# Routing digits and comparison results laid out token tile by token tile, with each digit written twice

## The chip, the core and the metric

The kernel runs on one core of a Trainium2 chip. The metric is the device time of one execution in microseconds (us); lower is better. TensorE (PE) multiplies matrices, VectorE (DVE) and ScalarE (ACT) work element by element, GpSimd (POOL) does some of that and the indirect DMAs, and SyncE's queue (SP) issues most other DMAs. Each engine takes its instructions in order from its own queue and waits on semaphores.

## The reference

Three stages follow one another. Attention: 4 batches, 8 heads, 576 positions, head dimension 64, half of the heads with a local window of 32, half with a strided mask. Its output is the x of 2304 tokens by 512. Then a layer with a cosine gate, and then a mixture of 8 experts whose tokens are assigned greedily under a capacity of 288:

```python
h = x @ w_in
x = (h * np.cos(h)) @ w_out
logits = x @ w_gate                          # 2304 x 8
order = np.argsort(-logits.flatten())
for idx in order:
    tok, e = idx // E, idx % E
    if assigned[tok] >= 0 or counts[e] >= cap:
        continue
    assigned[tok] = e
    counts[e] += 1
for e in range(E):
    mask = assigned == e
    out[mask] = np.maximum(x[mask] @ w1[e], 0.0) @ w2[e]
```

## The kernel before, in words

Tokens lie in 18 tiles of 128 (NC = 18): token 128 c + p is partition p, column c. Products of float32 accuracy are made of three float16 products (high and low parts). The instructions are first put into a plan (`Plan`, line 159) as groups with an engine, a nominal time, and the buffers that they read and write. `Plan.order` (line 192) simulates the engines on these nominal times and writes out one fixed list per engine; of the groups that could start, an engine takes the one with the longest way to the end. What the chip then does is wait, not choose. All matmuls go through `mm` (line 343, recorded as L358), all VectorE work through `Vec` (line 387, recorded as L392), activations through `act` (L382).

The stretch that matters here is the routing (`route`, line 1021), between the last logits and the first gather. The greedy assignment is done in 7 phases (loop over `ph`, line 1088), and each finds the logit at which one expert is full. In a phase:

- `best()` (line 1079) finds each token's best open expert; `oh` is its one-hot code (line 1090). It is copied 16 times side by side into `ohr` [128, NC, 16, NE], tiles 0 to 11 on VectorE (line 1091) and 12 to 17 on ScalarE (line 1092), so that `ohr[:, c]` is a stationary operand of 128 columns.
- The threshold is found digit by digit, 5 times (NIT, loop over `it`, line 1097). `d` holds one float16 digit per token (lines 1096 and 1114), `io` the 34 digit values (NDIG) to compare with, built once (line 1087). The compare `gq` (line 1099) says for every token and digit value whether the token's digit reaches it: 34 x 18 = 612 elements per partition.
- The product (line 1106): 18 matmuls, one per token tile, each with `ohr[:, c]` as the stationary and `gq[:, :, c]` as the moving operand (34 columns), add up in PSUM how many tokens of each expert reach each digit value. In the old layout [NDIG, NC] the 34 elements of a tile lie 18 elements apart.
- VectorE compares the counts with the room left (line 1108; in the trace TENSOR_SCALAR_CACHE_REDUCE and DVE_READ_ACCUMULATOR), transposes and takes the maximum (lines 1110 and 1111), and computes the next digit (line 1114). Here the next step begins. The result of the compare goes from VectorE to TensorE, that of the product back to VectorE, and so on: a chain.
- After the fifth digit, lines 1120 to 1143 settle ties and mark the expert as full.

Between the routing's products TensorE's list holds the second layer of the cosine stage (`l2_tile`, line 986): per token tile 48 products of up to 128 rows with 512 columns, tiles 5 to 17, in groups of `L2_GROUP` = 2 matmuls. They fill the time in which the chain is on VectorE. Their results are scaled on ScalarE, split on VectorE or GpSimd, and stored as `y_dram`.

In the same stretch `expert_weights` (line 1190) brings weights through two staging buffers `wst`: a DMA of 512 KB on SP, then for each half a rounding to float16 on ScalarE (line 1205) and the rest by a subtraction on VectorE (line 1206, SCALAR_TENSOR_TENSOR 128x512). A buffer is loaded again when both halves are subtracted. Expert 0's weights come at the routing's beginning, expert 1's at its end, since they take the memory of a part of the hidden layer. Expert 0's tokens are gathered (line 1219) when the routing has written the indices `idx` (line 1184).

Of the kernel before, what the change touches and what calls it, by code (L numbers as in the profile page):

```python
# [11 lines left out]
F16 = mybir.dt.float16  # L12
# [5 lines left out]
ALU = mybir.AluOpType  # L18
# [4 lines left out]
B, H, S, D = 4, 8, 576, 64  # L23
# [28 lines left out]
# changes of priority, by label  # L52
# [43 lines left out]
# engines that differ from the first one offered at a place  # L96
# [62 lines left out]
class Plan:  # L159
    """Instructions in groups, each on one engine, with the buffers that they read and write.  # L160
    order() lists them by a simulated schedule: of the groups that could start, an engine takes
    the one with the longest way to the end."""

    # from the end of a group to the start of one that needs it
# [42 lines left out]
    def reuse(self, old, new):  # L207
        """Buffers whose names start with one of `new` take the memory of those of `old`."""
        keys = [k for k in self.writer if k[0] in old]
        i = self.add(None, 0.0, None, w=keys)  # L210
        for k in keys:
            del self.writer[k], self.readers[k]
        for n in new:
            self.base[n] = i
        return i

    def order(self):
# [41 lines left out]
        def pe_end(i, at):  # L259
            """TensorE's clock is halved after a window with little activity, until one with much"""  # L260
            warm_ns = t[i][1]
            cold_ns, a = self.busy[i]
            left = 1.0
            while left > 1e-9:
                win = int(at / self.WINDOW + 1e-9)
                look(win)
                ns = warm_ns if warm[win] else cold_ns
                dt = min(left * ns, (win + 1) * self.WINDOW - at)
                active[win] += (a if warm[win] else 2.0 * a) * dt / ns
                left -= dt / ns  # L270
                at += dt
            return at
# [62 lines left out]
def kernel(ctx: ExitStack, tc: tile.TileContext, a: dict, out: bass.AP):  # L335
# [4 lines left out]
    # ------------------------------------------------------------ instructions  # L340
    def mm(group, r, w):
        """group: (out, lhsT, rhs, start, stop) each"""
        ns = cold = act_ns = 0.0
        for o, l, x, _, _ in group:
            k, m, n = l.shape[0], l.shape[1], size(x)
            if x.dtype == F32:
                one = 0.88 * n + 19.5 if k == 64 else max(n, m) / 0.6 * (1.0 if m > 64 else 0.76)
                cold += 2.0 * one
                act_ns += n / 0.6 * (1.0 if m > 64 else 0.5) * k / 128.0
            else:  # L350
                one = n / 9.6 + 15.0 if m <= 32 < n else n / 4.8 + 12.5 if m <= 64 < n else max(n / 2.4 + 3.0, 25.0)
                cold += max(2.0 * one - 6.0, 27.0)
                act_ns += n / 2.4 * k / 128.0
            ns += one

        def emit():
            for o, l, x, start, stop in group:
                nc.tensor.matmul(o, l, x, start=start, stop=stop)  # L358

        p.add("pe", ns, emit, r, w, busy=(cold, act_ns))  # L360
# [26 lines left out]
    class Vec:  # L387
        """Calls on the vector engine: dve.op(n, keys read, keys written, *args)"""
# [9 lines left out]
    def choose(site, *engines):  # L398
        """the engine of a place in the program: the first one named if CHOICE has no other"""
        return CHOICE.get(site, engines[0])  # L400

    def vtt(site, o, x, y, op, r, w, first="pool"):
        """a tensor_tensor on Pool or DVE"""
        if choose(site, *(("pool", "dve") if first == "pool" else ("dve", "pool"))) == "pool":
            ptt(o, x, y, op, r, w)
        else:
            dve.tensor_tensor(size(o), r, w, o, x, y, op=op)

    def low(site, o, x, scale, hi, xk, r, w, first="pool"):
        """o = scale * x - hi; on Pool it leaves scale * x in x"""  # L410
        if choose(site, *(("pool", "dve") if first == "pool" else ("dve", "pool"))) == "pool":
            pscale(x, x, scale, r, xk)
            ptt(o, x, hi, ALU.subtract, r, w)
        else:
            dve.scalar_tensor_tensor(size(o), r, w, o, x, scale, hi, op0=ALU.mult, op1=ALU.subtract)
# [7 lines left out]
    def ecopy(site, o, x, r, w, *engines):  # L423
        """a copy on the first of the engines if CHOICE has no other"""
        how = choose(site, *engines)
        if how == "pool":
            p.add("pool", 146.0 + 3.28 * size(o), lambda: nc.gpsimd.tensor_copy(o, x), r, w)
        elif how == "dve":
            dve.tensor_copy(size(o) // (2 if site[0] == "og" else 1), r, w, o, x)
        else:  # L430
            acopy(o, x, r, w)
# [10 lines left out]
    def dma_t(o, x, r, w):  # L442
        """16-bit transpose of blocks of 128 columns"""
        p.add("sp", 112.0 * x.shape[1] / 128, lambda: nc.sync.dma_start(o, x, transpose=True), r, w)

    # ------------------------------------------------------------------ memory
# [58 lines left out]
    # the clock of TensorE rises before the first products  # L505
# [3 lines left out]
    # --------------------------------------------------------------- attention  # L509
# [59 lines left out]
    def masks(pv, i0, i1, np_, local, o=2 * LK):  # L569
        """the start of a bank of scores: 8 times the mask"""  # L570
# [10 lines left out]
    def softmax(b, pr, scores, pv, sbk, halves, sv, sk, scale, norm):  # L581
        """sv = norm * softmax(scale * scores), keys sk + (0 or 1,)"""
# [106 lines left out]
    def att_half_load(b, pr):  # L689
        """as att_load, and the operands in float16 parts"""  # L690
# [18 lines left out]
    def att_half(b, pr):  # L709
        """att_pair with products of float16 parts"""  # L710
# [84 lines left out]
    # ----------------------------------------------------------------- weights  # L795
    def to_f32(site, dst, words, sk, ck):
        """The float32 of float64 given as its two 32-bit words."""
# [72 lines left out]
    # --------------------------------------------------------------- layer one  # L870
# [54 lines left out]
    def g_segments(t0, n):  # L925
        """tokens t0 .. t0+n-1 as (tile, offset, length, keys of a layer unit)"""
# [10 lines left out]
    # ------------------------------------------------------------------ logits  # L937
    def logits(c0, take, after=()):
        """gate logits of tokens 128 c0 .. 128 c0 + 383, straight from the hidden layer"""
# [22 lines left out]
    def early_logits(c, ys, yi, take):  # L962
        """gate logits of tokens 128 c .. 128 c + 127 from their rows of y; the rows are transposed into a free part of x"""
# [19 lines left out]
    # --------------------------------------------------------------- layer two  # L983
    yss, yfs = [], []

    def l2_tile(c, take, nf=2):
        """y rows 128c .. 128c+127, in float16 parts"""
# [32 lines left out]
    # ----------------------------------------------------------------- routing  # L1020
    def route(take, take_t):
        """Greedy assignment under the capacity: in every phase the tokens left go, best logit
        first, to their best open expert until one expert is full; the phase finds the logit at
        which that happens.  Then the tokens of each expert get slots, and idx their inverse."""

        def t(name, shape, dt=F32):
            return take(shape, dt)
# [42 lines left out]
        ds = [t("d", [128, NC], F16) for _ in range(2)]  # L1070
        eq, oh = t("eq", full), t("oh", full, F16)
        nt, nm, ne = t("nt", [128, 32]), t("nm", [128, 1]), t("ne", [128, 1])
        reach, io = t("reach", [128, NDIG]), t("io", [128, NDIG, NC], F16)
        gqs = [t("gq", [128, NDIG, NC], F16) for _ in range(2)]
# [12 lines left out]
        D(TS, 612, ["cb"], ["io"], io, cb[:, RC_J:RC_J + NDIG, None].to_broadcast([128, NDIG, NC]), 1520.0, None, op0=ALU.add)  # L1087
        for ph in range(NE - 1):
# [4 lines left out]
            # the logit of the token that fills an expert, digit by digit: the float16 of 1536 + x  # L1093
            # has x rounded to a whole number, -16 .. 16 in the part of the range that is looked at
            di, d = rot("d", ds)
            D(TS, NC, ["m"], [("r", "d", di)], d, m, 32.0, 1536.0, op0=ALU.mult, op1=ALU.add)
            for it in range(NIT):
                gi, gq = rot("gq", gqs)
                D(TT, 306, [("r", "d", di), "io"], [("gq", gi)], gq, d[:, None, :].to_broadcast([128, NDIG, NC]), io, op=ALU.is_ge)
# [6 lines left out]
                mm([(pc[:, :NDIG], ohr[:, c].rearrange("p a b -> p (a b)"), gq[:, :, c], c == 0, c == NC - 1) for c in range(NC)],  # L1106
# [5 lines left out]
                if it + 1 < NIT:  # L1112
                    di, d = rot("d", ds)
                    D(TS, 66, ["u", "nm"], [("r", "d", di)], d, u, nm, -32.0, op0=ALU.add, op1=ALU.mult)
# [8 lines left out]
            D(TS, 66, [("r", "d", di), "nm"], ["tie"], tie, d, nm, 1519.0, op0=ALU.subtract, op1=ALU.is_equal)  # L1123
            D(RED, NE, ["ce"], ["e8"], e8, ce, axis=AX.X, op=ALU.max)
            D(TT, 1, ["rem", "cv"], ["rem"], rem, rem, cv, op=ALU.subtract)
            D(TS, 66, [("r", "d", di), "nm"], ["sure"], sure, d, nm, 1520.0, op0=ALU.subtract, op1=ALU.is_ge)
# [62 lines left out]
    # ----------------------------------------------------------------- experts  # L1189
# [123 lines left out]
    # ---------------------------------------------------------------- the plan  # L1313
# [198 lines left out]
```

## Time and profile before

| | us |
|---|---|
| three runs | 814.16 (median), 814.12, 816.64 |
| span of the profiled execution | 813.8 |
| its routing, from the first digit product to the index product | 399.35 to 575.82 |

The profile's page gives no time of the profiled execution beside its span, which goes from its first to its last instruction; the median of the runs is 0.36 us above it. Stages are read best from a table of busy time per stretch. A row of a timeline gives the start, the length, the engine, the line, the operation, what it writes and reads, and how many consecutive instructions are merged into it. A matmul's recorded duration contains its way through the array, so consecutive ones overlap: the time from start to start is the merged length less the last one's duration, divided by the count less one.

### The profile page before, as it was taken

How to read it: one execution, taken by the hardware profiler on the slowest of the kernel's cores; microseconds unless marked ns; L12 is line 12 of the kernel's file. 1: busy time of each engine (PE TensorE's matmuls, PEld its weight loads, DVE VectorE, ACT ScalarE, POOL GpSimd, SP SyncE). 2: the span in 40 equal slices, each digit the busy share in tenths (PEclk: the TensorE clock that was granted, in tenths of full speed). 3: DMA queues.
4: the chain of work that ended last, by engine and by line, in shares of the span. 5: the costliest groups of instructions: out<-in, count | busy, mean ns of one | idle time of the engine just before them, and what ended most of it. 6: DMA issues, size and time to landing. Idle time of an engine off the chain costs nothing.

```text
span 813.8 us, 18700 instructions
## 1 busy us (share of the span) xinstructions
PE 739.8 (91%) x7520; PEld 519.7 (64%) x7520; DVE 527.3 (65%) x1356; ACT 410.9 (50%) x907; POOL 277.2 (34%) x292
## 2 busy tenths in 40 slices
PE   7878888989889989999999999999899989888896
PEld 5666666755444767877555565445787767666685
DVE  5899999984856788555685655458435556544620
ACT  3557778865734889788220000023135554554632
POOL 2766466856520364344010000000531343231231
PEclk9999999999999999999999999999999999999998
DMA  9954155654766722002330000006498999978731
GB/s 262 271 163 145 53 134 128 155 130 122 156 159 166 169 48 62 2 1 64 105 130 14 28 14 14 14 14 183 128 186 213 241 257 218 224 234 227 177 70 40
DMA packets 114262, 104.14 MB, mean 128 GB/s; under 512 B 79872, under 2 KB 89856, under 8 KB 114176
## 3 DMA queue, kind: packets, MB, share of 16 engines
q1 hardware_dynamic: 111104, 93.52, 45.0%
q0 software_dynamic: 3072, 9.44, 3.9%
q8 instruction: 59, 0.97, 0.5%
q14 instruction: 27, 0.22, 0.1%
HBM read 74.36 MB, written 9.70 MB: 103 GB/s over the span
## 4 chain that ended last, share of the span: by engine, by line
PE 40%; DMA 21%; DVE 20%; ACT 11%; issue 4%; POOL 3%; SPq 0%; POOLq 0%; DVEq 0%; ACTq 0%
PE psum L358 38%; DMA ar_l<-w 14%; DVE ar_t L392 7%; DVE ar_l L392 7%; ACT ar_l L382 5%; DVE ar_a L392 2%; ACT ar_t L382 2%; DVE ar_w L392 2%; ACT ar_a L382 2%; DMA ar_l<-ar_t 1%; DMA ar_a<-q 1%; DVE mxs L392 1%; DMA ar_w<-ar_w 1%; DMA ar_t<-w_out 1%; ACT L382 1%
## 5 line engine op out<-in xcount | busy, mean ns | idle before, releaser
L358 PEld LDWEIGHTS <-ar_l 128*128 128x128 f16 x2576 | 234.9, 100 | 102.4 <-issue 35.4
L358 PE MATMUL psum<-ar_l 128*128 128x288 f16 (+2 forms) x1578 | 206.9, 287 | 20.0 <-DVE ar_l L392 19.5
L358 PEld LDWEIGHTS <-ar_a 128*128 128x128 f16 (+1 forms) x1600 | 128.4, 99 | 90.4 <-issue 36.5
L358 PE MATMUL psum<-ar_w,ar_a 128*128 128x512 f16 (+3 forms) x1056 | 173.9, 308 | 6.3 <-DVE ar_w L392 2.8
L382 ACT ACTIVATE ar_l<-psum 128x288 int32<-128x288 f32 (+5 forms) x201 | 78.5, 413 | 111.7 <-PE psum L358 97.9
L358 PEld LDWEIGHTS <-ar_t 128*128 128x128 f16 (+2 forms) x1980 | 97.0, 107 | 43.5 <-issue 18.5
L392 DVE SCALAR_TENSOR_TENSOR ar_l<-ar_l,psum 128x288 f32<-128x288 int32 (+2 forms) x236 | 98.0, 440 | 34.4 <-ACT ar_l L382 33.1
L382 ACT ACTIVATE ar_a<-ar_l 128x512 f16<-128x512 f32 (+2 forms) x125 | 63.6, 537 | 55.6 <-DMA ar_l<-w 50.5
L392 DVE SCALAR_TENSOR_TENSOR ar_l<-ar_l 128x512 f16<-128x512 f32 (+3 forms) x94 | 52.3, 576 | 33.4 <-ACT ar_l L382 32.6
L382 ACT ACTIVATE ar_l<-ar_l,quarter 128x288 f32<-128x288 f32 x128 | 66.2, 531 | 13.0 <-DVE ar_l L392 12.2
L392 DVE SCALAR_TENSOR_TENSOR ar_t<-ar_t 128x512 uint32<-128x512 uint32 (+6 forms) x60 | 61.9, 1034 | 14.1 <-ACT ar_t L382 14.1
L437 POOL TENSOR_TENSOR ar_l<-ar_l 128x288 f32<-128x288 f32 (+1 forms) x41 | 27.8, 680 | 119.2 <-DVE ar_l L392 89.0
L392 DVE SCALAR_TENSOR_TENSOR ar_a<-ar_l,ar_a 128x512 f16<-128x512 f32 x64 | 43.5, 710 | 36.1 <-ACT ar_a L382 36.1
L358 PE MATMUL psum<-ar_w,ar_t 128*128 128x512 f16 (+2 forms) x288 | 65.4, 357 | 0.0
L382 ACT ACTIVATE ar_l<-ar_l 128x512 f16<-128x512 f32 x64 | 37.0, 622 | 53.3 <-DMA ar_l<-w 53.2
L382 ACT ACTIVATE ar_t<-ar_t 128x512 uint32<-128x512 uint32 (+12 forms) x63 | 46.4, 755 | 34.4 <-DVE ar_t L392 10.0
L358 PE MATMUL psum<-ar_b,ar_l 128*128 128x96 f16 (+1 forms) x576 | 54.4, 259 | 8.7 <-ACT ar_b L382 4.9
L358 PE MATMUL psum<-ar_w,ar_b 128*128 128x512 f16 (+1 forms) x240 | 61.5, 388 | 0.0
L358 PE MATMUL psum<-ar_b,ar_a 128*128 128x288 f16 (+3 forms) x504 | 53.4, 272 | 4.9 <-DVE ar_w L392 3.8
L358 PE MATMUL psum<-ar_w,ar_l 128*128 128x288 f16 x384 | 49.6, 292 | 3.8 <-DVE ar_w L392 3.8
L1296 POOL DMA_INDIRECT out<-ar_b,idx x24 | 23.5, 979 | 85.0 <-DMA out<-ar_b,idx 19.1
L392 DVE SCALAR_TENSOR_TENSOR ar_w<-psum,ar_w 128x288 f16<-128x288 f32 x64 | 28.0, 451 | 32.0 <-ACT ar_w L382 31.7
(142 smaller groups left out, 915.6 us busy)
## 6 DMA issues: line engine op xcount, KB each, us to landing
ar_l<-w SPq DMA_DIRECT2D x64, 512.0 KB
ar_t<-w_out SPq DMA_DIRECT2D x16, 512.0 KB
ar_t<-w_in SPq DMA_DIRECT2D x12, 512.0 KB
y_dram<-ar_l SPq DMA_DIRECT2D x13, 256.0 KB
ar_t<-vl SPq DMA_DIRECT2D x6, 432.0 KB
ar_t<-qs SPq DMA_DIRECT2D x4, 648.0 KB
ar_t<-vs SPq DMA_DIRECT2D x6, 384.0 KB
ar_t<-ql SPq DMA_DIRECT2D x4, 576.0 KB
```

What stands on the lines that cost most here:

```text
L358: nc.tensor.matmul(o, l, x, start=start, stop=stop)
L382: p.add("act", ns, lambda: nc.scalar.activation(o, x, func, **kw), r, w, tab=tab)
L392: p.add("dve", 69.0 + 1.042 * n, lambda: getattr(nc.vector, name)(*args, **kw), r, w)
L437: p.add("pool", 145.0 + (rate or (1.667 if y.dtype == F32 else 1.885)) * size(o), lambda: nc.gpsimd.tensor_tensor(o, x, y, op=op), r, w)
L1296: p.add("pool", 546.0, lambda og=og, T=T: nc.gpsimd.indirect_dma_start(out[:, :], bass.IndirectOffsetOnAxis(ap=idx[:, T:T + 1], axis=0), o ...
```

## The change

The layout of the table `io` and of the compare results `gq` becomes [NC, NDIG], token tile by token tile, so that the moving operand `gq[:, c, :]` is 34 elements in one piece. The digits `d` become [NC, 2]: each is written twice side by side, from an operand that is read with each element repeated (`twice`). The compare reads `d` as [NC, 17, 2], with the pair of equal digits repeated 17 times, and `gq` and `io` as 17 pairs per tile (`pairs`). The two later uses of the digits read every other element. The nominal times of the two digit instructions grow by 18 and by 18 elements. Blank lines also take the place of comments, which is left out here.

```diff
@@ route @@
-        ds = [t("d", [128, NC], F16) for _ in range(2)]
+        ds = [t("d", [128, NC, 2], F16) for _ in range(2)]
...
-        reach, io = t("reach", [128, NDIG]), t("io", [128, NDIG, NC], F16)
-        gqs = [t("gq", [128, NDIG, NC], F16) for _ in range(2)]
+        reach, io = t("reach", [128, NDIG]), t("io", [128, NC, NDIG], F16)
+        gqs = [t("gq", [128, NC, NDIG], F16) for _ in range(2)]
...
-        D(TS, 612, ["cb"], ["io"], io, cb[:, RC_J:RC_J + NDIG, None].to_broadcast([128, NDIG, NC]), 1520.0, None, op0=ALU.add)
+        D(TS, 612, ["cb"], ["io"], io, cb[:, None, RC_J:RC_J + NDIG].to_broadcast([128, NC, NDIG]), 1520.0, None, op0=ALU.add)
+        pairs = lambda x: x.rearrange("p c (j h) -> p c j h", h=2)
+        twice = lambda x: x[:, :, None].to_broadcast([128, NC, 2])
         for ph in range(NE - 1):
...
-            D(TS, NC, ["m"], [("r", "d", di)], d, m, 32.0, 1536.0, op0=ALU.mult, op1=ALU.add)
+            D(TS, 2 * NC, ["m"], [("r", "d", di)], d, twice(m), 32.0, 1536.0, op0=ALU.mult, op1=ALU.add)
             for it in range(NIT):
                 gi, gq = rot("gq", gqs)
-                D(TT, 306, [("r", "d", di), "io"], [("gq", gi)], gq, d[:, None, :].to_broadcast([128, NDIG, NC]), io, op=ALU.is_ge)
+                D(TT, 306, [("r", "d", di), "io"], [("gq", gi)], pairs(gq),
+                  d[:, :, None, :].to_broadcast([128, NC, NDIG // 2, 2]), pairs(io), op=ALU.is_ge)
...
-                mm([(pc[:, :NDIG], ohr[:, c].rearrange("p a b -> p (a b)"), gq[:, :, c], c == 0, c == NC - 1) for c in range(NC)],
+                mm([(pc[:, :NDIG], ohr[:, c].rearrange("p a b -> p (a b)"), gq[:, c, :], c == 0, c == NC - 1) for c in range(NC)],
                    [("gq", gi), ("fit", 0), ("fit", 1)], kc)
...
-                    D(TS, 66, ["u", "nm"], [("r", "d", di)], d, u, nm, -32.0, op0=ALU.add, op1=ALU.mult)
+                    D(TS, 2 * NC + 48, ["u", "nm"], [("r", "d", di)], d, twice(u), nm, -32.0, op0=ALU.add, op1=ALU.mult)
...
-            D(TS, 66, [("r", "d", di), "nm"], ["tie"], tie, d, nm, 1519.0, op0=ALU.subtract, op1=ALU.is_equal)
+            D(TS, 66, [("r", "d", di), "nm"], ["tie"], tie, d[:, :, 0], nm, 1519.0, op0=ALU.subtract, op1=ALU.is_equal)
...
-            D(TS, 66, [("r", "d", di), "nm"], ["sure"], sure, d, nm, 1520.0, op0=ALU.subtract, op1=ALU.is_ge)
+            D(TS, 66, [("r", "d", di), "nm"], ["sure"], sure, d[:, :, 0], nm, 1520.0, op0=ALU.subtract, op1=ALU.is_ge)
```

## Rows read from the trace of the kernel before

**Rows 1.** The page's busy time per engine: us, share of the span, instructions.

```profile
PE 739.8 (91%) x7520; PEld 519.7 (64%) x7520; DVE 527.3 (65%) x1356; ACT 410.9 (50%) x907; POOL 277.2 (34%) x292
```

**Rows 2.** Busy time by stretch, of the routing; columns as in the first row.

```profile
core 0: us, PE busy (x) PEld busy (x) DVE busy (x) ACT busy (x) POOL busy (x), PEclk, DMA share, GB/s
395.00:575.80 180.80, 178.16 (x1313) 98.45 (x1313) 119.25 (x535) 31.47 (x53) 12.49 (x21) 1.00 0.20 65
```

**Rows 3.** The chain of waits in order of time: start, us, what; its longest pieces.

```profile
393.06 45.59 PE psum L358 x340
...
442.12 114.28 PE psum L358 x850
```

**Rows 4.** Matmuls by shape, 385 to 600 us: busy us, mean ns, idle before.

```profile
L358 PE MATMUL psum<-ar_l,ar_t 128*128 128x34 f16 x630 | 45.6, 242 | 0.0
...
L358 PE MATMUL psum<-wp,ar_t 128*128 128x16 f16 x52 | 3.3, 172 | 0.0
L358 PE MATMUL psum<-wp,ar_t 128*128 128x8 f16 x52 | 3.2, 166 | 0.0
```

**Rows 5.** Timeline of one search step, 449.5 to 453.1 us.

```profile
449.75 1.31 PE L358 MATMUL psum<-ar_l,ar_t 128*128 128x34 f16 x18
...
450.88 2.34 PE L358 MATMUL psum<-ar_w,ar_a 128*128 128x512 f16 x10
451.10 0.25 DVE L392 TENSOR_SCALAR_CACHE_REDUCE ar_l<-psum,ar_l 128x33 f32<-128x33 f32 x1 [0.97 <-PE psum L358]
...
451.87 0.35 DVE L392 TENSOR_SCALAR ar_l<-ar_l 128x18 f16<-128x18 f32 x2
452.14 0.48 DVE L392 TENSOR_TENSOR ar_l<-ar_l 128x612 f16<-128x612 f16 x1
...
453.06 0.22 PE L358 MATMUL psum<-ar_l,ar_t 128*128 128x34 f16 x1
```

**Rows 6.** Timeline of TensorE: logits (16 and 8 columns in turn) and expert 0 (96 columns).

```profile
267.40 0.34 PE L358 MATMUL psum<-wp,ar_b 128*128 128x16 f16 x8
...
584.06 2.04 PE L358 MATMUL psum<-ar_b,ar_l 128*128 128x96 f16 x44
```

**Rows 7.** The chain of waits, 540 to 600 us.

```profile
558.24 3.99 DMA ar_l<-w
...
562.91 0.69 DVE ar_a L392
...
564.45 4.67 DMA ar_l<-w
...
569.81 0.69 DVE ar_a L392
...
575.16 0.62 DVE ar_l L392
575.78 0.04 issue
575.82 5.69 PE psum L358 x46
```

**Rows 8.** VectorE by shape, 395 to 578 us: busy us, mean ns, idle before.

```profile
L392 DVE TENSOR_TENSOR ar_l<-ar_l 128x612 f16<-128x612 f16 x35 | 16.7, 477 | 0.3
...
L392 DVE TENSOR_TENSOR ar_l<-ar_l 128x144 f32<-128x144 f32 x16 | 4.9, 303 | 0.2
...
L392 DVE TENSOR_TENSOR ar_t<-ar_t 128x1728 f16<-128x1728 f16 x1 | 1.9, 1944 | 0.0
```

**Rows 9.** Timeline of a phase's beginning, 425 to 455 us.

```profile
445.34 0.83 ACT L385 COPY ar_t<-ar_l 128x768 f16<-128x768 f16 x1 [5.15 <-DVE ar_l L392]
...
446.45 1.30 PE L358 MATMUL psum<-ar_l,ar_t 128*128 128x34 f16 x18
```

**Rows 10.** Timelines of VectorE, ScalarE and TensorE in the last phase.

```profile
550.36 0.68 DVE L392 SCALAR_TENSOR_TENSOR ar_a<-ar_l,ar_a 128x512 f16<-128x512 f32 x1
...
556.82 0.69 DVE L392 SCALAR_TENSOR_TENSOR ar_a<-ar_l,ar_a 128x512 f16<-128x512 f32 x1
...
556.16 1.15 ACT L382 ACTIVATE ar_a<-ar_l 128x512 f16<-128x512 f32 x2 [1.81 <-DMA ar_l<-w]
...
551.97 1.31 PE L358 MATMUL psum<-ar_l,ar_t 128*128 128x34 f16 x18
```

## The prediction, made before the change was timed

> **What bounds the kernel now.** I read the page's busy shares first, then the busy time of stages, the chain of waits, and last the timeline of one search step. The page says that TensorE is busy for 91% of an 813.8 us span [rows 1]. That is an average; the change touches only the routing, so the stage is what counts. [...] The chain of waits runs through TensorE alone for 45.59 us and then for 114.28 us in this stretch [rows 3]. So while the routing searches for its thresholds, TensorE's queue ends last: it holds the layer-two products of the cosine layer and, slipped in between them in a fixed order, the routing's own products. What shortens TensorE's list in this stretch shortens the kernel, as long as the routing's chain on VectorE stays within what TensorE has to do anyway.
>
> **What the routing costs TensorE.** There are 7 phases of 5 digit searches, so 35 products of 18 matmuls with 34 columns: the 630 rows of the group [rows 4]. One product begins at 449.75 and the layer-two matmul behind it at 450.88 [rows 5]: 1.13 us for 18 matmuls, 0.063 each. Its moving operand is read with a step of 18 elements (36 bytes), since a column of one token tile is strided in the old layout. The 35 products take 39.6 us of TensorE.
>
> How fast could such a matmul be? In the kernel's logits, matmuls of 16 and 8 columns, read without a gap and each with a fresh 128x128 stationary operand, run as a group of eight in 0.34 us, of which the last one's duration is 0.17: 0.17 / 7 = 0.024 us from start to start [rows 4, 6]. Matmuls of 96 columns without a gap, also with a fresh 128x128 operand, run 44 in 2.04 us with some 0.21 for the last one: 0.043 each [rows 6]. Thirty-four columns lie near 16 and far from 96, and the time of neither is proportional to its columns. I take 0.025. A product is then 18 x 0.025 = 0.45, and 0.04 for the change to the next 512-column matmul: 0.49 us in place of 1.13, a saving of 0.64. With 0.043 each it would be 0.81 and the saving 0.32. The bounds are thus nothing and 0.64 us a product; the least is what remains if the stride is not the cause.
>
> [...] The rows show 0.063 us a matmul for 34 strided columns and 0.024 for 16 in one piece. [...]
>
> **What the change costs VectorE.** One search step, followed through [rows 5]: the last matmul of the product starts at 450.82 (449.75 + 1.31 less its own 0.24), VectorE's comparison with the room left starts at 451.10, and after the transpose, the maximum and the new digit (451.87) the 612-element compare ends at 452.62. The next product starts at 453.06. TensorE needs 0.05 us from the end of a VectorE result to its start (575.78 to 575.82, where it stood idle) [rows 7]. So the step's chain has 453.06 - 452.62 - 0.05 = 0.39 us to spare under ten layer-two matmuls (2.34 us in the timeline, the last one overlapping). Of the 28 steps inside phases 19 have this pattern, the others have 12 to 16 matmuls there.
> - Digits written twice: 18 to 36 elements, between nothing and 18 x 1.1 ns, the dearest rate below: 0.02 us at most. It is in the chain, so in the slack. I take 0.02.
> - The compare: the number of elements is the same. Now it takes 0.477 us [rows 8], with the digit row of 18 read again and again. A compare whose one operand repeats each single element takes 1.944 us for 1728 elements, 1.125 ns each [rows 8], so 0.69 for 612. The paired digits keep an innermost run of two elements; I take 0.48, with 0.69 as the upper bound: 0.21 more, still inside the 0.39. A gain is excluded as far as the time goes: the chain is covered.
> - The product's last matmul also ends sooner: 34 columns in one piece should last about as long as the logits' 16 (0.17) rather than 0.242 [rows 4], so the chain begins some 0.06 earlier. Slack and gain grow together.
> - The table of comparison digits is built once, before the routing, and the two reads of every other digit at a phase's end are 18 elements as before: nothing, under layer-two work.
> - The first product of a phase waits for the repeated one-hot copies; ScalarE's ends at 446.17 and the product starts at 446.45 [rows 9]. The compare ended long before. Nothing changes there.
> No DMA, no wait and no queue position is added. The list order is computed from nominal costs, which grow by 19 ns per digit; a pair of layer-two matmuls may move by one step, which leaves TensorE's sum as it is.
>
> **What is late next.** Of the 35 products 33 lie before VectorE's subtraction at 550.36 us, and two behind it (551.97 is the first) [rows 10]: 33 x 0.64 = 21.1 us. Behind that, expert 1's weights get into the chain: two staging buffers, each loaded, rounded by ScalarE and subtracted by VectorE in VectorE's fixed order, with the routing's last steps queued behind the subtractions. Already now the subtraction at 556.82 begins the moment its ScalarE half is there (556.16 and 0.6), and the loads of 3.99 and 4.67 us follow in the chain with the subtractions at 562.91 and 569.81 [rows 7, 10]. The load that the subtraction at 556.82 waits for could be issued only once the one at 550.36 had emptied its buffer, so the saving of the two last products (1.3 us) finds the weights no earlier: I keep 0.06 of it, from the earlier start of the chain. In phase 0, where expert 0's weights share VectorE in the same way, I take off 0.3, a guess between nothing and one step's 0.64. Sum: 21.1 + 0.06 - 0.3 = 20.9 us. From 575.8 on nothing has a fixed start: gathers, expert weights and stores are released by what came before, so the rest moves as a block. Against the span that gives 813.8 - 20.9 = 792.9 us. The median of the runs is 814.16, 0.36 above the profiled span, so I predict 793.3 us.
>
> **Rivals.**
> - Partial: a matmul keeps 0.043 us, the figure of 96 columns [rows 6]. Then 35 x 0.32 = 11.2 us, less 0.6 at the weights: 814.16 - 10.6, about 803.5. Against it: 34 is far nearer to 16. Chance 0.06.
> - Nothing: 0.063 has another cause than the stride, a floor of issue for instance, and the change does not do what it says on TensorE. The compare stays in its slack, so 814.2. Against it: the 0.024 of the logits in the same queue [rows 6]. [...] Chance 0.06.
> - Slower, by one mechanism: the compare has to start anew at each of its 306 pairs. In a step the chain would then be product 0.45, about 1.73 from the last matmul's start to the compare's end, 0.05, and the excess x: 2.23 + x, against 3.31 us from start to start now (449.75 to 453.06). It decides from x = 1.08 us, so from 0.69 + 306 r - 0.48 = 1.08, r = 2.8 ns a pair. At 5 ns x is 1.74 and 28 steps lose 0.66 each: 814.2 + 18.5 = 832.7. Against it: a multiplication in rows of 8 takes 0.303 us for 144 elements [rows 8], with no visible charge per row; no row shows rows of two. Chance 0.03.
>
> **How the numbers follow.** My forecast has 0.85, the partial rival 0.06, no change 0.06, slower 0.03. Faster by over 0.3% (2.4 us, about what a measurement of this kernel can tell from no change) is 0.85 + 0.06 = 0.91; same 0.06; slower 0.03. The low end takes 35 full savings with nothing given back (22.4 us) and 0.06 in some twenty steps (1.2 us): 790.5. The high end takes the forecast with 0.030 us a matmul (35 x 18 x 0.005 = 3.2 us less), 1.5 us more lost at the weights of experts 0 and 1 (what I take off there, once more), and 2.0 us for a list whose pairs fall out worse (five pairs of 0.43 us: ten matmuls take 2.18 us from 450.88 to 453.06 [rows 5]): 800. The other three cases, 0.15 together, stay outside.
>
> **What would show it.** The 34-column group should fall from 0.242 to about 0.18 us a matmul, and a product from 1.13 to 0.5 us; the compare should stay at 0.48 us and the ten 512-column matmuls follow at once, with TensorE never idle inside a phase; the step should be some 2.67 us; the index product should come near 555 us. More waiting of VectorE for the weights of expert 1 should appear at the end of the routing. I am wrong on TensorE if the product keeps 1.1 us, and wrong on VectorE if the compare exceeds 0.87 us, for then gaps open before the products.

## The result, and the profile after

The changed kernel takes 795.37 us (median of four runs, 794.81 to 796.68), the kernel before in the same session 815.4: a ratio of 0.976 with a 95% interval of 0.9725 to 0.9796. Measured twice more beside the experiments it is 0.9736 [0.9685, 0.9788] and 0.973 [0.9686, 0.9774]. The forecast of 793.3 for 814.16 is a ratio of 0.974, so faster, and by about as much as forecast.

Read in the order of the prediction: first the page's busy shares of the kernel after, to be held against [rows 1].

```profile
PE 717.5 (90%) x7520; PEld 497.4 (63%) x7520; DVE 527.4 (66%) x1356; ACT 409.7 (52%) x907; POOL 275.7 (35%) x292
```

TensorE has lost 22.3 us of work (739.8 to 717.5) and VectorE none (527.3 to 527.4), with the same counts of instructions. The next view, matmuls by shape from 385 to 600 us, says where; it answers to [rows 4].

```profile
L358 PE MATMUL psum<-ar_l,ar_t 128*128 128x34 f16 x630 | 21.3, 178 | 0.6 <-DVE ar_l L392 0.6
...
L358 PE MATMUL psum<-wp,ar_t 128*128 128x16 f16 x52 | 3.4, 174 | 0.0
L358 PE MATMUL psum<-wp,ar_t 128*128 128x8 f16 x52 | 3.3, 167 | 0.0
```

The 630 digit matmuls fell from 242 to 178 ns each, and as a group from 45.6 to 21.3 us; the logits' 16 and 8 columns beside them did not move. The timeline of two search steps (start, length, engine) shows the rest; it answers to [rows 5].

```profile
449.70 0.61 PE L358 MATMUL psum<-ar_l,ar_t 128*128 128x34 f16 x18
...
450.16 2.32 PE L358 MATMUL psum<-ar_w,ar_a 128*128 128x512 f16 x10
450.35 0.25 DVE L392 TENSOR_SCALAR_CACHE_REDUCE ar_l<-psum,ar_l 128x33 f32<-128x33 f32 x1 [0.55 <-PE psum L358]
...
451.11 0.36 DVE L392 TENSOR_SCALAR ar_l<-ar_l 128x36 f16<-128x36 f32 x2
451.39 0.48 DVE L392 TENSOR_TENSOR ar_l<-ar_l 128x612 f16<-128x612 f16 x1
...
452.31 0.61 PE L358 MATMUL psum<-ar_l,ar_t 128*128 128x34 f16 x18
...
452.77 2.32 PE L358 MATMUL psum<-ar_w,ar_a 128*128 128x512 f16 x10
```

From start to start a digit matmul now takes (0.61 - 0.178) / 17 = 0.025 us. A product (449.70 to 450.16) takes 0.46 us in place of 1.13, and a step of product and ten layer-two matmuls (449.70 to 452.31) 2.61 in place of 3.31. VectorE's compare still takes 0.48. It ends at 451.87, 0.44 us before the product that needs it; before it was 452.62 and 453.06 [rows 5], the same 0.44.

Now the sum. The busy time of the routing, from the first digit product to the index product, first of the kernel before, then after (us, then the engines, TensorE's granted clock, DMA share, GB/s):

```profile
399.35:575.82 176.47, 173.81 (x1293) 96.38 (x1292) 115.45 (x522) 29.63 (x51) 12.51 (x21) 1.00 0.19 61
```

```profile
402.90:558.92 156.02, 151.34 (x1301) 73.69 (x1300) 115.95 (x522) 29.62 (x51) 12.61 (x21) 1.00 0.21 68
```

The routing is 20.45 us shorter. It hardly differs between executions: 156.0, 156.2 and 156.5 us in the three profiles of the changed kernel, 176.5 and 177.2 in the two with the old layout. TensorE's work in it falls by 22.47 us, not by the 35 x 0.67 = 23.5 of the products, since eight more layer-two matmuls of 256 columns now lie ahead of the index product (74 in place of 66, 10.2 us in place of 9.2, in the same view by shape). Its idle time grows from 2.66 to 4.68 us. So 23.5 - 1.0 - 2.0 = 20.5.

| profiled executions, us | before | after | difference |
|---|---|---|---|
| start to first digit product | 399.35 | 402.90 | +3.55 |
| routing | 176.47 | 156.02 | -20.45 |
| index product to the end | 237.98 | 235.38 | -2.60 |
| span | 813.8 | 794.3 | -19.5 |

The first and third lines are not the routing's. Up to the first digit product both kernels have the same lists of instructions, some 2.3 of the 3.55 us have arisen by 275 us, and in the other profiles of this case the product begins between 398.75 and 403.42 us. For the third line, TensorE's timeline behind the index product, before and after:

```profile
576.61 5.10 PE L358 MATMUL psum<-ar_w,ar_t 128*128 128x256 f16 x30
...
584.06 2.21 PE L358 MATMUL psum<-ar_b,ar_l 128*128 128x96 f16 x48
```

```profile
559.71 2.56 PE L358 MATMUL psum<-ar_w,ar_t 128*128 128x256 f16 x22
...
567.25 4.04 PE L358 MATMUL psum<-ar_b,ar_l 128*128 128x96 f16 x48
```

Here 30 matmuls were left before and 22 after, and in the kernel before the granted clock fell in this stretch (0.72 as a mean over 575.82 to 582.00; after, 0.99 over 558.92 to 565.00): 2.54 us. But they are lost again, since the changed kernel then waits 2.0 us for expert 0's gathers: expert 0's first product begins 8.24 us behind the index product before and 8.33 after. The 2.60 us come from the layer that begins there, and what follows takes the same time (busy time, before and then after):

```profile
584.06:601.49 17.43, 14.76 (x299) 14.12 (x297) 5.23 (x11) 4.29 (x11) 6.92 (x7) 0.90 0.73 136
601.49:813.80 212.31, 186.72 (x1648) 147.08 (x1645) 97.80 (x183) 103.65 (x229) 58.79 (x72) 0.97 0.77 191
```

```profile
567.25:581.93 14.68, 14.68 (x300) 14.68 (x298) 4.55 (x10) 4.29 (x11) 6.44 (x7) 0.85 0.77 147
581.93:794.30 212.37, 184.41 (x1648) 145.55 (x1645) 97.19 (x183) 103.23 (x229) 58.53 (x72) 0.98 0.77 192
```

In that layer TensorE stood idle for 2.67 us before and not at all after. The timeline names no engine that it waited for, and no run shows that the change is the cause: from the index product to the end, the profiles of the kernels here that leave expert 1's loads in their place take from 233.4 to 239.6 us, and one with the old layout (e4 below) takes 234.5.

Last the chain of waits of the kernel after, against [rows 3, 7]:

```profile
405.28 4.33 DMA ar_l<-w
...
411.70 4.11 DMA ar_l<-w
...
421.26 15.40 PE psum L358 x151
...
440.14 88.92 PE psum L358 x767
...
534.44 5.22 DMA ar_l<-w
...
547.59 4.28 DMA ar_l<-w
...
552.56 0.69 DVE ar_a L392
...
558.92 3.15 PE psum L358 x38
```

From 421 to 530 us TensorE still bounds the search in the main. At both ends the weights have entered the chain. Two loads of expert 0's weights now stand in it in phase 0, where before it ran through TensorE alone [rows 3], and the loads of expert 1's weights enter at 534 us, 24 us ahead of the index product; before, it was at 558, 18 us ahead of it. Phase 0 became shorter by only 2.05 us (24.75 to 22.70), not by five products' 3.35; TensorE's timeline shows a wait at its end that was not there before:

```profile
421.26 0.17 PE L358 MATMUL psum<-ar_l 128*128 128x18 f16 x1 [1.10 <-DVE ar_l L392]
```

### The profile page after: what moved, and what is told of

The parts are those of the page before. It is cut to its first block, busy times and chain, and to the rows that moved or that the text cites. A ratio compares the mean times of both kernels' runs of the same rounds, so it can differ in the third digit from the quotient of the medians.

```text
span 794.3 us, 18699 instructions
## 1 busy us (share of the span) xinstructions
PE 717.5 (90%) x7520; PEld 497.4 (63%) x7520; DVE 527.4 (66%) x1356; ACT 409.7 (52%) x907; POOL 275.7 (35%) x292
## 4 chain that ended last, share of the span: by engine, by line
PE 33%; DMA 26%; DVE 22%; ACT 12%; issue 4%; POOL 2%; SPq 1%; POOLq 0%; ACTq 0%; DVEq 0%
PE psum L358 32%; DMA ar_l<-w 14%; DVE ar_l L392 9%; DVE ar_t L392 7%; ACT ar_l L382 5%; DVE ar_a L392 3%; ACT ar_a L382 2%; ACT ar_t L382 2%; DMA ar_t<-w_in 2%; DVE ar_w L392 2%; DMA ar_b<-ar_b 1%; DMA ar_l<-ar_t 1%; DMA ar_b<-y_dram,idy 1%; DVE mxs L392 1%; DMA ar_t<-w_out 1%
## 5 line engine op out<-in xcount | busy, mean ns | idle before, releaser
L358 PEld LDWEIGHTS <-ar_t 128*128 128x128 f16 (+4 forms) x1980 | 74.6, 101 | 42.3 <-issue 19.0
L358 PE MATMUL psum<-ar_w,ar_t 128*128 128x512 f16 (+2 forms) x288 | 63.8, 349 | 0.0
L358 PE MATMUL psum<-ar_b,ar_a 128*128 128x288 f16 (+3 forms) x504 | 55.2, 277 | 8.1 <-DVE ar_w L392 4.2
L358 PE MATMUL psum<-ar_b,ar_l 128*128 128x96 f16 (+1 forms) x576 | 51.2, 253 | 6.6 <-ACT ar_b L382 3.4
L358 PE MATMUL psum<-ar_w,ar_l 128*128 128x288 f16 x384 | 47.9, 286 | 3.5 <-DVE ar_w L392 3.5
L437 POOL TENSOR_TENSOR ar_t<-ar_t 128x512 uint32<-128x512 uint32 (+7 forms) x25 | 40.5, 1623 | 20.5 <-ACT ar_t L382 19.9
```

The lines of the kernel that those rows point to most:

```text
L437: p.add("pool", 145.0 + (rate or (1.667 if y.dtype == F32 else 1.885)) * size(o), lambda: nc.gpsimd.tensor_tensor(o, x, y, op=op), r, w)
```

## The experiments

**How near must the elements lie?** The theory is that a digit matmul waits for its moving operand because of the distance between elements, and that VectorE's side is covered. Three kernels and the changed kernel as their yardstick, on one chip (the kernel before: 818.2 us).

> The changed kernel again, as the measure for the three beside it. Both theories: 793 to 797 us, a product of 0.46 us from its first matmul to the next layer-two matmul.

Measured: 797.29 us, ratio 0.9736 [0.9685, 0.9788].

The first writes each digit once and lets the compare repeat it 34 times in place of pairs, with the new layout otherwise.

```diff
-        ds = [t("d", [128, NC, 2], F16) for _ in range(2)]
+        ds = [t("d", [128, NC], F16) for _ in range(2)]
...
-                D(TT, 306, [("r", "d", di), "io"], [("gq", gi)], pairs(gq),
-                  d[:, :, None, :].to_broadcast([128, NC, NDIG // 2, 2]), pairs(io), op=ALU.is_ge)
+                D(TT, 306, [("r", "d", di), "io"], [("gq", gi)], gq,
+                  d[:, :, None].to_broadcast([128, NC, NDIG]), io, op=ALU.is_ge)
...
```

> Only the layout is kept: each digit is written once, and the compare repeats every single digit 34 times. TensorE's list is the same, instruction for instruction. Theory (TensorE's list ends last, the chain on VectorE has some 0.4 us to spare in a step): the product stays at 0.46 us, the compare goes from 0.48 us to 0.69 us or up to 0.79 us, and the time stays within 1.5 us of the changed kernel. Rival (the chain is what ends last, the pairs are needed): 28 steps times 0.2 to 0.3 us, 6 to 9 us slower than the changed kernel.

Measured: 798.45 us, ratio 0.9747 [0.9696, 0.9799]. Its TensorE group by shape, and its timeline of a compare:

```profile
L358 PE MATMUL psum<-ar_l,ar_t 128*128 128x34 f16 x630 | 21.3, 177 | 1.7 <-DVE ar_l L392 1.6
```

```profile
452.91 0.80 DVE L392 TENSOR_TENSOR ar_l<-ar_l 128x612 f16<-128x612 f16 x1
453.84 0.61 PE L358 MATMUL psum<-ar_l,ar_t 128*128 128x34 f16 x18
```

The matmuls gain the same with or without pairs. The compare costs 0.80 us, 0.32 more than in pairs, and ends 0.13 us before its product starts: the slack swallows it. The routing takes 157.29 us (403.20 to 560.48), 1.3 more. The pairs thus keep the compare fast, but in this kernel that is worth about 1 us, inside the interval.

The other two keep the digits once and interleave the results of 2 or of 6 token tiles, so that a tile's elements lie 4 or 12 bytes apart, against 2 after the change and 36 before (`GT` is 2 or 6).

```diff
...
-        gqs = [t("gq", [128, NC, NDIG], F16) for _ in range(2)]
+        gqs = [t("gq", [128, NC // GT, NDIG, GT], F16) for _ in range(2)]
...
-                mm([(pc[:, :NDIG], ohr[:, c].rearrange("p a b -> p (a b)"), gq[:, c, :], c == 0, c == NC - 1) for c in range(NC)],
+                mm([(pc[:, :NDIG], ohr[:, c].rearrange("p a b -> p (a b)"), gq[:, c // GT, :, c % GT], c == 0, c == NC - 1) for c in range(NC)],
...
```

> Two token tiles interleaved: the 34 elements of a moving operand are 2 elements (4 bytes) apart in place of 18 (36 bytes) before and 1 in the changed kernel; each digit is written once and the compare runs over pairs of two tiles. The list is the changed kernel's. Theory (the distance between elements sets the matmul's time, a small one is cheap): 0.025 to 0.035 us a matmul, time within 6 us of the changed kernel, between 793 and 801 us. Rival (what counts is only whether the operand lies in one piece): 0.063 us a matmul as before, 811 to 815 us. [...]

> Six token tiles interleaved: elements 12 bytes apart, otherwise as the kernel with two. Theory (the distance sets the time): between the two, 0.035 to 0.063 us a matmul and 798 to 814 us. Rival (only one piece or not counts): 0.063 us a matmul, 811 to 815 us. [...]

Measured: two tiles 796.36 us, ratio 0.9733 [0.9687, 0.978]; six tiles 807.76, ratio 0.9851 [0.9786, 0.9915]. The matmuls by shape, and a product in the timeline, of two tiles and then of six:

```profile
L358 PE MATMUL psum<-ar_l,ar_t 128*128 128x34 f16 x630 | 21.3, 178 | 0.9 <-DVE ar_l L392 0.8
452.31 0.61 PE L358 MATMUL psum<-ar_l,ar_t 128*128 128x34 f16 x18
```

```profile
L358 PE MATMUL psum<-ar_l,ar_t 128*128 128x34 f16 x630 | 36.5, 227 | 0.6 <-DVE ar_l L392 0.6
...
452.72 1.03 PE L358 MATMUL psum<-ar_l,ar_t 128*128 128x34 f16 x18
```

At 4 bytes a matmul still takes 0.025 us from start to start, at 12 bytes (1.03 - 0.227) / 17 = 0.047, at 36 bytes 0.0625 (products of 1.30 and 1.31 us in the kernel before, less 0.242, by 17). So the distance is the cause. A floor of issue would not know these steps: with it the kernel with 12 bytes would have kept the 0.0625. That rules out the rival "nothing" by more than the result alone. Two tiles side by side keep the compare at its old 0.48 us too, without writing any digit twice: the same gain by another road.

**Is part of the gain the new order of the list?** The change also raises two nominal times, and with them the order may change. One kernel is the old one with the new nominal times, the other the new one with the old nominal times. One of the two lines that the first changes:

```diff
...
-                    D(TS, 66, ["u", "nm"], [("r", "d", di)], d, u, nm, -32.0, op0=ALU.add, op1=ALU.mult)
+                    D(TS, 2 * NC + 48, ["u", "nm"], [("r", "d", di)], d, u, nm, -32.0, op0=ALU.add, op1=ALU.mult)
```

> The kernel before with only the two nominal times of the change (19 ns more for a digit), so the old layout with the changed kernel's order of instructions. Theory (the gain is the shorter matmul): same as before within 2.4 us, about 814 us. Rival (the new order is part of the gain): 3 us or more faster than the kernel before.

> The changed kernel with the old nominal times, so the new layout with the order of instructions of the kernel before. Theory (the gain is the shorter matmul): same as the changed kernel within 2.4 us, about 795 us. Rival (the new order is part of the gain): 797 us or more, by as much as the new order alone gains on the old layout.

Measured: the old kernel with the new times 815.55 us, ratio 0.9993 [0.9967, 1.0019]; the new kernel with the old times 794.17, ratio 0.9728 [0.969, 0.9765]. The routing takes 177.2 and 155.4 us in their profiles. Against 176.5 before and 156.0, 156.2 and 156.5 in the changed kernel, the new order costs the routing some 0.6 to 1.0 us. In the time of the whole kernel that cannot be told from nothing.

**Does the compare have slack, and how much?** In the next kernel it is issued three times in a row, as one entry of the plan, so that TensorE's list stays as it is.

```diff
-                D(TT, 306, [("r", "d", di), "io"], [("gq", gi)], pairs(gq),
-                  d[:, :, None, :].to_broadcast([128, NC, NDIG // 2, 2]), pairs(io), op=ALU.is_ge)
+                def thrice(gq=gq, d=d):
+                    for _ in range(3):
+                        nc.vector.tensor_tensor(pairs(gq), d[:, :, None, :].to_broadcast([128, NC, NDIG // 2, 2]), pairs(io), op=ALU.is_ge)
+                p.add("dve", 69.0 + 1.042 * 306, thrice, RK("io") + [("r", "d", di)], [("gq", gi)])
```

> The changed kernel with every compare issued three times into the same place, as one entry of the plan, so that TensorE's list stays the changed kernel's. Each repeat adds some 0.39 us to the chain of a step (from start to start of consecutive instructions), 0.78 us in all. Theory (a step of ten layer-two matmuls has 0.39 us to spare, one of twelve 0.85 us): the 16 steps with ten lose 0.39 us each, those with twelve nothing, three steps in phase 0 and two in phase 6 with little to spare 0.4 to 0.8 us each, together 9 to 10 us: about 805 us where the changed kernel takes 795 us. Rival (the chain already ends last): 28 steps lose 0.78 us, 22 us, about 817 us.

Measured: 817.07 us, ratio 0.9971 [0.9942, 0.9999], a miss for the theory's number. The TensorE group by shape with its waits, and two steps of the timeline:

```profile
L358 PE MATMUL psum<-ar_l,ar_t 128*128 128x34 f16 x630 | 21.3, 177 | 17.0 <-DVE ar_l L1105 9.7 <-DVE ar_l L392 5.3 <-DVE ar_t L392 1.8
...
453.94 1.50 DVE L1105 TENSOR_TENSOR ar_l<-ar_l 128x612 f16<-128x612 f16 x3
...
455.50 0.60 PE L358 MATMUL psum<-ar_l,ar_t 128*128 128x34 f16 x18 [0.47 <-DVE ar_l L1105]
455.95 2.32 PE L358 MATMUL psum<-ar_w,ar_a 128*128 128x512 f16 x10
...
458.76 0.40 PE L358 MATMUL psum<-ar_l,ar_t 128*128 128x34 f16 x10 [0.50 <-DVE ar_l L392]
```

Steps of twelve layer-two matmuls lie elsewhere in the same timelines, two starts in the changed kernel and then two here:

```profile
505.63 0.61 PE L358 MATMUL psum<-ar_l,ar_t 128*128 128x34 f16 x18
508.70 0.61 PE L358 MATMUL psum<-ar_l,ar_t 128*128 128x34 f16 x18
```

```profile
525.41 0.60 PE L358 MATMUL psum<-ar_l,ar_t 128*128 128x34 f16 x18
528.65 0.60 PE L358 MATMUL psum<-ar_l,ar_t 128*128 128x34 f16 x18
```

Each repeat took 0.51 us (three in 1.50), more than the 0.39 I had reckoned. That lengthens the chain by 1.02. Less a slack of 0.39 a step of ten matmuls should grow by 0.63, and less one of 0.85 a step of twelve by 0.17, both to 3.24 us; without slack they would grow by 1.02, to 3.63 and 4.09. Of the 16 steps of ten, 15 grew from 2.61 to between 3.24 and 3.28 (455.50 to 458.76 above), and the six steps of twelve between phase 0 and the long compare from 3.07 to between 3.24 and 3.27. So the slack is there, and of the size that was read. The rival gave nearly this total without a slack; the lengths of the steps, not the total, tell the two apart. The recorded idle time is no measure of it: it is mostly 0.47 us in front of a product behind ten matmuls and 0.01 behind twelve, some 0.17 less than each step grew, since the last matmul's record runs on beyond the start of the next. In the changed kernel the record of ten from 450.16 lasts 2.32 us, to 452.48, and the product behind it starts at 452.31, 0.17 earlier. The routing grew by 18.7 us (to 174.7): 10.7 in the 16 steps, 1.1 in the six, 3.9 in the rest of phase 0, and the rest in the last phase and at the ends of phases.

**The one long compare.** In the changed kernel 34 compares take 0.48 us and one 1.43. Its timeline:

```profile
530.63 1.19 POOL L437 TENSOR_TENSOR ar_l<-ar_t,ar_l 128x512 f16<-128x512 f32 x1 [9.99 <-ACT ar_t L382]
530.72 1.43 DVE L392 TENSOR_TENSOR ar_l<-ar_l 128x612 f16<-128x612 f16 x1
532.21 0.60 PE L358 MATMUL psum<-ar_l,ar_t 128*128 128x34 f16 x18 [0.56 <-DVE ar_l L392]
```

A subtraction on GpSimd (the low part of token tile 13) runs from 530.63 to 531.82, and the compare, begun 0.09 us later, ends only 0.33 us after it; TensorE waits 0.56. The next kernel gives this tile's split (13) to VectorE.

```diff
...
-    ('ylo', 14): 'dve',
+    ('ylo', 13): 'dve', ('ylo', 14): 'dve',
...
```

> The changed kernel with one choice changed: the low part of token tile 13 is computed on VectorE in place of GpSimd. In the changed kernel one compare of the 35 takes 1.43 us while that GpSimd instruction runs (530.63 to 531.82 us), and TensorE then stands idle for 0.56 us. Theory (the two engines hinder each other): all 35 compares take 0.47 to 0.48 us and that idle time goes; the time changes by less than a measurement can tell. Rival (something else delays that one): a compare over 1 us remains.

Measured: 797.92 us, one execution. Its compares by shape:

```profile
L392 DVE TENSOR_TENSOR ar_l<-ar_l 128x612 f16<-128x612 f16 x35 | 16.7, 476 | 0.2
```

No long one is left (mean 476 ns against 504), so the overlap with GpSimd made it. The order matters. In all the profiles of this case ten compares begin while a subtraction on GpSimd runs, and all ten take 1.31 to 1.75 us. Five begin shortly before one and keep 0.47 or 0.48 us; one of them is in the kernel before:

```profile
413.83 0.47 DVE L392 TENSOR_TENSOR ar_l<-ar_l 128x612 f16<-128x612 f16 x1
...
413.92 1.40 POOL L437 TENSOR_TENSOR ar_l<-ar_t,ar_l 128x512 f16<-128x512 f32 x1 [30.71 <-ACT ar_t L382]
```

The long compare came with the new order of the list and not with the layout: the old layout with the new list (e4) has it, the new layout with the old list (e5) has not (compares of 503 and 475 ns as a mean). In e8 the routing is no shorter without it, 155.97 us (400.44 to 556.41), since a product a little later waits for the experts' weights in its place (1.2 us of idle time in front of the digit products, 0.6 in the changed kernel).

**What do expert 1's weights cost?** One kernel holds all loads of expert 1 back until the indices are there, the other only those of its second half, `w2`. The edit of the first; in the second the condition is `e == 1 and name == "w2"`:

```diff
-                    a[name][e, 128 * k:128 * (k + kk), :].rearrange("(k p) f -> p k f", p=128), 524288, [], [("wst", si)])
+                    a[name][e, 128 * k:128 * (k + kk), :].rearrange("(k p) f -> p k f", p=128), 524288, [("idy",)] if e == 1 else [], [("wst", si)])
```

> The changed kernel, but the loads of expert 1's weights wait for the routing's indices, so that none of their subtractions stands in VectorE's list ahead of the index product. Theory (the routing's end is held by the weights in VectorE's list): from the first digit product to the index product 153 to 154.5 us in place of 156.0 us in the changed kernel, and VectorE never waits for ScalarE's halves of expert 1 before it; the whole kernel is slower all the same, 797 to 815 us, since the eight loads of 512 KB come some 25 us later. Rival (the weights only fill gaps): 155.5 to 156.5 us.

> The changed kernel once more, as the yardstick of the next run on the same chip: 794 to 799 us, ratio 0.973 to 0.977 to the kernel before.

> Only the second half of expert 1's weights (w2) waits for the indices; w1 is brought inside the routing as in the changed kernel. Theory (the weights inside the last phases cost the routing time, but what comes too late costs the experts' stage as much): the routing, from the first digit product to the index product, takes some 150 to 153 us, between 156.0 (changed kernel) and 146.8 (all of expert 1's weights late), and if expert 0 covers four loads and their eight halves, the whole gains 3 to 6 us on the changed kernel: 791 to 794. Rival (the staging buffers and VectorE are full in the experts' stage too, so every late load is paid back there): 796 to 799, no gain.

Measured: all late 796.01 us, ratio 0.9724 [0.9673, 0.9776]; w2 late 799.79 (793.72 to 802.92) beside the changed kernel's 797.15 (793.83 to 801.58) on that chip. The busy time of the two stages, routing and rest, in three fences: the changed kernel, w2 late, all late.

```profile
403.42:559.88 156.46, 151.30 (x1302) 73.65 (x1300) 116.00 (x522) 29.74 (x51) 12.28 (x21) 1.00 0.21 68
559.88:793.30 233.42, 205.31 (x2020) 164.46 (x2019) 105.10 (x199) 108.89 (x241) 71.80 (x84) 0.97 0.76 188
```

```profile
398.75:549.73 150.98, 147.77 (x1270) 70.54 (x1268) 110.89 (x514) 25.83 (x45) 10.33 (x20) 1.00 0.17 55
549.73:791.70 241.97, 208.10 (x2054) 168.54 (x2052) 109.43 (x207) 112.28 (x248) 73.10 (x85) 0.97 0.76 191
```

```profile
401.29:548.13 146.84, 145.09 (x1253) 68.92 (x1252) 106.64 (x506) 19.68 (x33) 10.28 (x20) 1.00 0.13 42
548.13:791.80 243.67, 210.29 (x2069) 168.53 (x2067) 114.57 (x215) 118.26 (x259) 73.83 (x85) 0.98 0.78 198
```

The routing is 5.5 (w2 late) and 9.6 us (all late) shorter, the second more than I expected, and the rest 8.6 and 10.3 us longer, longer also than in any of the other profiles here (233.4 to 239.6). Routing and rest together are 389.88, 392.95 and 390.51 us; in the two other profiles of the changed kernel they are 391.4 and 392.3. The rest moves its data with a DMA share of 0.76 to 0.78, in which the late loads must find their place; with w2 late TensorE also waits for expert 0's gathers, as its waits from 545 to 640 us show (in total, times, longest; 0.2 us in the changed kernel beside it, though 2.0 in its first profile):

```profile
PE psum L358 <- DMA ar_b<-y_dram,idx: 7.3, 3, 4.0
```

What the routing loses to the weights is therefore not free to be won: in these single profiles the experts' stage pays it back. In time neither version differs from the changed kernel by more than the noise: with all late it did not become slower, which I had expected, and with w2 late the gain of 3 to 6 us that the theory had did not come.

## Why the prediction was right, point by point

- **The matmul.** 0.025 us from start to start was taken from the logits, and it is 0.025; the upper bounds 0.043 and 0.063 play no part. The columns' distance in memory, not their number, was the cost, as e2 and e3 show. A floor of issue, which the rival "nothing" names as an instance, does not hold here: the same instruction takes 0.025, 0.047 and 0.0625 us at 4, 12 and 36 bytes. Why the time grows with the distance in this way no run shows. Between 4 and 12 bytes nothing was run.
- **The product.** 0.49 forecast, 0.46 measured: the change to the next matmul costs no 0.04. The 35 products gave 23.5 us where the sum had 22.4.
- **The compare** stayed at 0.48, in its slack, as taken. The bound of 0.69 for a compare that repeats single elements was too low: e1 has 0.80. It was scaled in proportion from an instruction of 1728 elements; between 612 and 1728 elements (0.80 and 1.94 us) the rate is 1.02 ns, which leaves, as an estimate from these two, 0.17 us that does not scale. The conclusion (inside the slack) still held, by 0.13 us.
- **The slack** was forecast to grow by 0.06; it stayed at 0.44 from the compare's end to the product's start. The chain from the last matmul's start to the compare's end did shorten, from 1.80 (450.82 to 452.62) to 1.74 (450.13 to 451.87), but TensorE's time from the same start to the next product shrank as much, from 2.24 to 2.18.
- **The list.** I left TensorE's sum as it is. Eight matmuls of 256 columns moved ahead of the index product, 1.0 us that the routing pays and that the work behind it is spared, and the one compare met GpSimd.
- **What is late next** was the right kind, too small, and put in the wrong place. I took off 1.5 us, and idle time grew by 2.0. The 0.3 for phase 0, a guess, measured 1.1: it is the wait at 421.26 for a chain that now runs through expert 0's loads. From phase 6 on, where I had put 1.2 at the weights of expert 1, idle time grew by 0.92 (2.21 to 3.13), and 0.56 of that is the compare that GpSimd stretched, which no step of the sum had and which breaks the sign "TensorE never idle inside a phase". VectorE's waits for ScalarE's halves grew at both experts, from 0.3 to 0.9 us and from 1.2 to 2.0 us in the groups by shape, and e8 shows that without the stretched compare TensorE waits for the weights in its place.
- **The sum** of the steps, 20.9, against a routing shorter by 20.45 and a span shorter by 19.5. That it came so near is in part luck: the products gave 1.1 us more than the sum had, the list took 1.0 and the idle time 0.5 more. The index product came at 558.92 and not near 555, since in this execution the search began 3.55 us later. That is no work of the change; why it differs so from one execution to another stays open.
- **The rest as a block.** The sum took the time behind the index product as unchanged. It was 2.6 us shorter, and as far as the runs show that is a difference between executions.
- **From span to time.** I set the median 0.36 us above the profiled span, but the two came from different executions. The profiled execution of the changed kernel took 796.68 us for a span of 794.3, so 2.4 us lie around a span, and the profiled execution before most likely took some 816 us. This step was wrong in form; in number it only put back 814.16 as the base. The forecast was low by 2.1 us: 0.8 of it is the saving, 20.0 us between the medians where 20.9 was forecast, well inside the interval, and 1.2 is the base, 815.4 with a fourth run in place of 814.16.
- **The rivals.** "Partial" and "nothing" fall with the 0.025 us. "Slower" needed a compare dearer by 1.08 us; e6 gave it 1.02 more and lost nearly the whole gain (ratio 0.9971), which fits that threshold, while pairs cost nothing (0.48 us, as before). The 5 ns a pair in its sum was an assumption of mine, which no run shows.

## What to carry to other kernels

Look at how far apart the elements of a small matmul's moving operand lie: with 34 columns, 36 bytes cost two and a half times what 2 or 4 bytes cost (0.0625 us against 0.025), and interleaving two tiles is enough to be rid of it. Before making one engine's work shorter, measure the slack of the chain beside it in the timeline, from the end of the result to the start of its reader: here 0.44 us hid a compare that became 0.32 us longer, and did not hide one longer by 1.0. And hold a stage's gain against the stage behind it, since a stall on prefetched weights may be the price of a shorter stage to come.

## What the runs showed that I had not expected

- The cost of a matmul of 34 columns grows with the distance of its elements: 0.025 us at 2 and at 4 bytes, 0.047 at 12, 0.0625 at 36.
- A VectorE compare of two operands that began while a GpSimd subtraction ran took 1.43 us in place of 0.48 (1.31 to 1.75 in the ten cases here); the five that began before one kept 0.47 or 0.48. Without that GpSimd instruction the long compare is gone (e8, mean 476 ns).
- The same compare repeated into the same destination takes 0.51 us from one to the next, where a different instruction follows it after 0.39.
- Holding back prefetches shortened the routing by up to 9.6 us and the kernel by nothing that can be told.
- In phase 0 a third of the saving, 1.1 of 3.35 us, was lost to the next thing to be late, the loads of expert 0's weights.
